# Two chained mixture-of-experts layers on one core: the branch on a job's width, the place of the output gates, the third gather and the row buffers are rewritten

## Chip, core and metric

One core of one Trainium2 chip. The metric is the device time of one launch in microseconds (us); several launches are timed and the median is used.

## What is computed

Local attention, then a mixture of 8 experts that routes by the largest logit, then a second mixture of 8 experts in which every expert takes exactly 576 tokens. All in float32; 4608 tokens, 512 columns, 1024 hidden columns. The reference, cut to the part around the change (the first expert layer):

```python
def _moe_ref(x, w_gate, w_output_gate, w1, w2):
    N, D = x.shape
    logits = x @ w_gate
    e_idx = np.argmax(logits, axis=1)
    logits_s = logits - logits.max(-1, keepdims=True)
    probs = np.exp(logits_s)
    probs /= probs.sum(-1, keepdims=True) + 1e-09
    gate_w = probs[np.arange(N), e_idx]
    eom = 1.0 / (1.0 + np.exp(-(x @ w_output_gate)))
    out = np.zeros((N, D), dtype=np.float32)
    for e in range(E):
        mask = e_idx == e
        h = np.maximum(x[mask] @ w1[e], 0.0)
        ye = h @ w2[e]
        out[mask] = gate_w[mask, None] * eom[mask, e, None] * ye
    return out
```

## The kernel before

The program has three stages. **Attention** walks over 36 blocks of 128 tokens, writes the rows to DRAM (`xs`), and beside it the router works out for each token its expert and a slot in a list (`route`, `plan`). The **first expert layer** works the list off in jobs: a job is one expert's block of tokens. The **second expert layer** (`moe2`) selects 576 tokens for each expert and runs the experts one after the other; the change leaves it alone.

**Jobs and widths.** Jobs 0 to 2 hold 256 tokens each and start before routing is complete. Jobs 3 to 10 take a full block of 256 and the rest of the same expert together, sorted by size, and are 512, 448, 384, 320 or 256 tokens wide. The width is known only when the router is done, so each of these jobs exists five times in the code, once for each width; one copy is called an arm here, arm 0 being 512 wide and arm 4 256 wide. Jobs from 11 on are 256 wide, one behind the other, each under a test whether there are that many jobs at all (`tail`). With the inputs timed here jobs 3 to 10 take arms 0, 1, 1, 2, 3, 3, 3, 4, and job 14 is the last.

**The branch.** `run` (L709) calls `arms` (L713), which writes a binary tree of tests on four numbers `wide[k]` (how many jobs are wider than a limit). Each engine holds these numbers in registers (L289 loads four of them and the number of jobs) and runs the tree for itself: a test whose body is taken goes on with the instruction behind it, otherwise it jumps to the other half. The five arms lie one behind the other in the code, arm 0 first; at the end of an arm each engine jumps to what follows the fifth arm. There `evac` (L878) copies the last quarter of the output out of PSUM, and the next job's tests follow.

**Inside a job.** `layer1` (L832) multiplies by w1: eight parts f, each 4 x 3 matmuls (every float32 operand is split into a high and a low half, `whi`/`wlo`, `xhi`/`xlo`, `hhi`/`hlo`). ACT makes `hhi` (L849), DVE `hlo` (L850). After every quarter a hook runs: it splits chunks of w2 (`split`, L694: ACT `whi` L697, DVE `wlo` L698) and fetches the same chunk of the next job's w1 into the raw buffer that came free (`fetch`, L687, a DMA issue on SP, L691). `layer2` (L859) multiplies by w2 in three groups of output quarters, and at the places given by `TODO` it splits the next job's w1, fetches the next job's w2 and turns and splits the next job's rows (L824, L829, L830).

**Gathers.** `x_load` (L811) works out row numbers on DVE (`idx`, L816) and issues indirect DMAs on POOL (L818) that gather a job's rows into `xr`. For jobs 1 and 2 it is called from a hook of the job before (L769), in job 0 at hook 0 and in job 1 at hook 1:

```python
            if i == (1 if j else 0) and j < EARLY - 1:
                self.x_load(n)
```

**Gates.** `gate(j-1)` (L886) is a generator that runs during `layer1` of job j, one step for every three matmuls. It multiplies the finished output `yT` by the second layer's gate weights (L894), copies that (`gT`, L896), turns it (L904), sets down logits and choices (`place`, `choose`: small DVE operations), and turns the output rows with DVE (`rows`: `y`, L916), each of two or four `y` followed by four stores to DRAM on SP (L919, `x<-y`). Its first step is one `yield`, so its first matmuls stand behind six matmuls of `layer1`. `y` comes from a pool with two buffers: the third transpose of a job waits until the stores of the first have landed.

PE, DVE, ACT and SP run their instructions in the order in which this code calls them; each engine's queue is strictly in that order.

Of the kernel before, what the change touches and what calls it, by code (L numbers as in the profile page):

```python
# [8 lines left out]
F32 = mybir.dt.float32  # L9
# [28 lines left out]
CH = 1024  # L38
SURE = NJ - E
EARLY = 3  # L40
HOLD = 1
GFULL = E * (BT - 1) // (128 * G)
TH = 2 * BT
STEP = 64
NC = (TH - BT) // STEP
CAP = N // E
BIG = 1e38
HC = 100
# [20 lines left out]
class Kernel:  # L69
# [136 lines left out]
    def setup(self, st):  # L206
        nc, tc = self.nc, self.tc
        dram = self.ctx.enter_context(tc.tile_pool(name="dram", bufs=1, space=DRAM))
        self.xs = dram.tile([N, D], F32, name="xs")
        self.list = dram.tile([NB * BT, 2], F32, name="list")  # L210
        self.x2 = dram.tile([NB * BT, ROW], F32, name="x2")
        keep = self.ctx.enter_context(tc.tile_pool(name="keep", bufs=1))
        self.seed = keep.tile([128, 2 * EARLY], I32, name="seed")
        self.jobs = keep.tile([128, 3], I32, name="jobs")
        self.counts = keep.tile([128, NC + 1], I32, name="counts")
        self.L = keep.tile([128, NS, E], F32, name="L")
        self.m = keep.tile([128, NS], F32, name="m")
        self.C = keep.tile([128, NS, E], BF, name="C")
        self.first = keep.tile([128, NS, 16], BF, name="first")
        self.f = keep.tile([128, NS], F32, name="f")  # L220
        self.left = keep.tile([128, 1], F32, name="left")
        self.dead = keep.tile([128, NS], F32, name="dead")
        wpool = self.ctx.enter_context(tc.tile_pool(name="weights", bufs=1))
        self.raw = [wpool.tile([128, CH], F32, name=f"wr{i}") for i in range(4)]
        self.chunks = self.weights(wpool, 0)
        self.ps = st.enter_context(tc.tile_pool(name="psA", bufs=1, space=PSUM))
        self.turn = self.ring = 0
        self.later = []
        self.last = None
        fix = st.enter_context(tc.tile_pool(name="fix", bufs=1))  # L230
        self.xr = fix.tile([128, 4, D], F32, name="xr")
        self.blank = fix.tile([128, ROW], F32, name="blank")
        self.meta = [fix.tile([128, 4, 2], F32, name=f"meta{i}") for i in range(3)]
        self.xhi = fix.tile([128, 4, TH], F32R, name="xhi")
        self.xlo = fix.tile([128, 4, TH], F32R, name="xlo")
        self.tab = fix.tile([128, E, NJ], F32, name="tab")
        self.order = fix.tile([128, E, EARLY], F32, name="order")
        self.opened0 = fix.tile([128, E, NJ], F32, name="opened0")
        self.total0 = fix.tile([128, 1], F32, name="total0")
        self.acc0 = fix.tile([128, E], BF, name="acc0")  # L240
        self.mw = st.enter_context(tc.tile_pool(name="mw", bufs=2))
        self.wk = st.enter_context(tc.tile_pool(name="wk", bufs=2))
# [36 lines left out]
    def first_layers(self):  # L279
        nc, tc = self.nc, self.tc  # L280
        self.consts = self.ctx.enter_context(tc.tile_pool(name="consts", bufs=1))
        with ExitStack() as st:
            self.setup(st)
            with ExitStack() as sa:
                self.attention(sa)
            self.buffers(st)
            for j in range(EARLY):
                self.job(j, BT)
            *self.wide, self.count = (nc.values_load(self.counts[0:1, i:i + 1], min_val=0, max_val=E if i < NC else NB)  # L289
                                      for i in range(NC + 1))  # L290
            for j in range(EARLY, SURE):
                self.run(j)
                self.evac()
            self.tail(SURE)
# [324 lines left out]
    def plan(self, cnt, used):  # L619
# [38 lines left out]
        yield  # L658
        V.tensor_reduce(pos, big, axis=AX.X, op=OP.add)
        V.tensor_scalar(cn[:, NC:], cn[:, NC - 1:NC], float(EARLY), None, op0=OP.add)  # L660
        V.tensor_copy(self.counts[:, 0:NC], cn[:, 0:NC])
        yield
        V.scalar_tensor_tensor(ct, pos[:, :, None].to_broadcast(sj), EARLY + 1.0, t1, op0=OP.add, op1=OP.mult)
        cp = wk.tile(sj, F32, name="pcp", bufs=1)
        V.tensor_tensor_scan(cp.rearrange(jf), pr.rearrange(jf), pr.rearrange(jf), initial=cn[:, NC:],
                             op0=OP.add, op1=OP.bypass)
        yield
        V.tensor_copy(self.counts[:, NC:], cp[:, E - 1, NJ - 1:NJ])
        V.tensor_tensor(cp, cp, pr, op=OP.mult)
        V.tensor_tensor(ct, ct, cp, op=OP.add)  # L670
        yield
# [36 lines left out]

    def run(self, j):  # L709
        self.last = self.ps.tile([128, TH if self.wideable(j) else BT], F32, name="tp2")  # L710
        self.arms(j, 0 if self.wideable(j) else NC, NC)

    def arms(self, j, lo, hi):  # L713
        if lo == hi:
            self.job(j, TH - STEP * lo)
            return
        k = (lo + hi) // 2
        with self.tc.If(self.wide[k] > j - EARLY) as cmp:
            self.arms(j, lo, k)
        with cmp.Else():  # L720
            self.arms(j, k + 1, hi)

    def tail(self, j):
        tc = self.tc
# [12 lines left out]
    def job(self, j, w):  # L737
# [21 lines left out]
        def hook1(i):  # L759
# [6 lines left out]
            elif j == EARLY - 2 and i == 3:  # L766
                while self.routes:
                    self.advance(1)
            if i == (1 if j else 0) and j < EARLY - 1:  # L769
                self.x_load(n)  # L770
            if i == 3:
                if EARLY - 2 <= j < NB - 2:
# [113 lines left out]
    def gate(self, j):  # L886
# [1 line left out]
        meta = self.meta[j % 3]  # L888
        n = 4 if self.wideable(j) else 2
        w = n * 128  # L890
        yield
        pg = self.ps.tile([128, w], F32, name="pg")
        for k in range(4):
            nc.tensor.matmul(pg[32 * k:32 * k + 32], self.wg2s[:, k, :], self.yT[:, k, 0:w], start=True, stop=True)  # L894
# [17 lines left out]

    def rows(self, u, s):
        nc = self.nc
        y = self.mw.tile([128, 4, 4, 32], F32, name="y")
        nc.vector.transpose(y, self.yT[:, :, u * 128:(u + 1) * 128].rearrange("p k (t g) -> p g k t", g=4))  # L916
        to = self.x2[s * 128:(s + 1) * 128, 0:D].rearrange("(t g) (q c) -> g q t c", g=4, q=4)
        for g in range(4):
# [504 lines left out]
```

## Time and profile before

| | |
|---|---|
| median of 3 launches | 1337.66 us (1333.54 to 1338.27) |
| profiled execution, its own time | 1333.46 us |
| span of its instructions | 1331.6 us |
| busy: PE, DVE, ACT, POOL | 87%, 58%, 37%, 14% of the span |
| mean granted TensorE clock | 0.926 of full speed |
| the chain that ended last | PE 57%, issue 14%, DVE 7%, DMA 5% |

The jobs of the first expert layer in that execution (PE's first matmul of the job, and how long PE had stood still before it):

| job | width | starts at us | PE idle before, us |
|---|---|---|---|
| 3 | 512 | 306.78 | 0.34 |
| 4 | 448 | 358.56 | 4.36 |
| 5 | 448 | 408.35 | 4.82 |
| 6 | 384 | 458.86 | 4.81 |
| 7 | 320 | 506.94 | 7.57 |
| 8 | 320 | 552.33 | 6.68 |
| 9 | 320 | 599.18 | 8.77 |
| 10 | 256 | 644.97 | 7.61 |
| 11 | 256 | 677.27 | 2.70 |

A row of a timeline gives start, duration, engine, line, operation, output and inputs, shape, count and, in brackets, how long the engine stood idle before it and what ended that; "issue" means that the engine waited for nothing that the profile shows. A clock of 1.0 is 2.4 GHz and 0.5 is 1.2 GHz. In the DMA view q8 and q14 are the queues that bring instructions: q8 moves 16 KB pieces and q14 8 KB pieces.

### The profile page before, as it was taken

How to read it: one execution, taken by the hardware profiler on the slowest of the kernel's cores; microseconds unless marked ns; L12 is line 12 of the kernel's file. 1: busy time of each engine (PE TensorE's matmuls, PEld its weight loads, DVE VectorE, ACT ScalarE, POOL GpSimd, SP SyncE). 2: the span in 40 equal slices, each digit the busy share in tenths (PEclk: the TensorE clock that was granted, in tenths of full speed). 3: DMA queues.
4: the chain of work that ended last, by engine and by line, in shares of the span. 5: the costliest groups of instructions: out<-in, count | busy, mean ns of one | idle time of the engine just before them, and what ended most of it. 6: DMA issues, size and time to landing. Idle time of an engine off the chain costs nothing.

```text
span 1331.6 us, 23258 instructions
## 1 busy us (share of the span) xinstructions
PE 1157.2 (87%) x8424; PEld 998.5 (75%) x8424; DVE 776.3 (58%) x2214; ACT 489.6 (37%) x1052; POOL 192.7 (14%) x233
## 2 busy tenths in 40 slices
PE   6978789689898896769789963999999999999997
PEld 4766568688697796768689952878797878788895
DVE  4756687855254354345366667767787868654430
ACT  4655454334242243234244421323232323334430
POOL 3112243111101101110000101020202021112001
PEclk8978789899998897888899975899999999999999
DMA  6776867765353554564467652241515052434310
GB/s 207 235 180 203 202 204 152 198 204 143 109 163 105 151 168 107 161 193 112 123 181 226 206 152 91 76 143 60 168 35 194 14 190 73 138 96 148 114 48 36
DMA packets 90581, 190.06 MB, mean 143 GB/s; under 512 B 22992, under 2 KB 46608, under 8 KB 90384
## 3 DMA queue, kind: packets, MB, share of 16 engines
q1 hardware_dynamic: 77904, 153.96, 39.9%
q0 software_dynamic: 11136, 32.59, 7.7%
q8 instruction: 97, 1.59, 0.6%
q10 hardware_dynamic: 1344, 1.10, 0.3%
q14 instruction: 100, 0.82, 0.2%
HBM read 152.33 MB, written 35.28 MB: 141 GB/s over the span
## 4 chain that ended last, share of the span: by engine, by line
PE 57%; issue 14%; DVE 7%; DMA 5%; POOL 1%; ACT 1%; SPq 1%; ACTq 0%; another core or an unknown queue 0%; POOLq 0%; DVEq 0%
PE O L844 6%; PE ph L844 5%; PE ph L1289 4%; PE ph L1293 4%; PE ph L1291 4%; PE py L1326 3%; PE py L1324 3%; PE py L1328 3%; DMA wr<-in_w_dram 2%; PE O L867 2%; PE O L869 2%; PE O L868 2%; PE ph L867 2%; PE ph L869 2%; PE ph L868 2%
## 5 line engine op out<-in xcount | busy, mean ns | idle before, releaser
L698 DVE TENSOR_TENSOR wlo<-wr,whi 128x1024 fp32r<-128x1024 f32 x122 | 146.6, 1218 | 39.1 <-ACT whi L697 38.4
L1289 PE MATMUL ph<-xhi,whi 128*128 128x256 f32 (+1 forms) x512 | 155.6, 304 | 2.0 <-DVE hlo L1298 0.7
L697 ACT ACTIVATE whi<-wr 128x1024 fp32r<-128x1024 f32 x122 | 126.5, 1054 | 80.8 <-DMA wr<-in_w_dram 37.4
L1291 PE MATMUL ph<-xlo,whi 128*128 128x256 f32 (+1 forms) x512 | 154.7, 302 | 0.0
L1293 PE MATMUL ph<-xhi,wlo 128*128 128x256 f32 (+1 forms) x512 | 154.4, 302 | 0.0
L818 POOL DMA_INDIRECT xr<-xs,idx x48 | 46.3, 965 | 461.9 <-DVE idx L816 143.1
L844 PE MATMUL O<-xhi,whi 128*128 128x256 f32 (+4 forms) x240 | 79.8, 334 | 33.6 <-issue 33.6
L1326 PE MATMUL py<-wlo,hhi 128*128 128x512 f32 x256 | 105.2, 411 | 0.0
L1328 PE MATMUL py<-whi,hlo 128*128 128x512 f32 x256 | 103.0, 402 | 0.0
L1324 PE MATMUL py<-whi,hhi 128*128 128x512 f32 x256 | 102.7, 401 | 0.0
L1297 ACT ACTIVATE hhi<-ph 128x256 fp32r<-128x256 f32 x128 | 49.0, 384 | 145.3 <-PE ph L1293 140.6
L1289 PEld LDWEIGHTS ph<-xhi,whi 128*128 128x128 f32 x512 | 98.5, 192 | 3.9 <-issue 1.1
L1291 PEld LDWEIGHTS ph<-xlo,whi 128*128 128x128 f32 x512 | 98.7, 193 | 0.5 <-DVE xlo L1260 0.2
L1293 PEld LDWEIGHTS ph<-xhi,wlo 128*128 128x128 f32 x512 | 98.5, 192 | 0.4
L844 PE MATMUL ph<-xhi,whi 128*128 128x256 f32 (+4 forms) x240 | 76.8, 324 | 14.1 <-issue 11.4
L1245 DVE TENSOR_TENSOR wlo<-wr,whi 128x512 fp32r<-128x512 f32 x124 | 81.9, 684 | 8.1 <-ACT whi L1240 8.1
L1298 DVE SCALAR_TENSOR_TENSOR hlo<-ph,hhi 128x256 fp32r<-128x256 f32 x128 | 53.0, 419 | 51.5 <-ACT hhi L1297 33.3
L844 PEld LDWEIGHTS O<-xhi,whi 128*128 128x128 f32 x240 | 47.6, 198 | 45.6 <-issue 44.5
L844 PE MATMUL O<-xhi,wlo 128*128 128x256 f32 (+4 forms) x240 | 77.0, 323 | 0.0
L844 PE MATMUL ph<-xhi,wlo 128*128 128x256 f32 (+4 forms) x240 | 74.5, 314 | 0.0
L403 PE MATMUL ph<-qkv 128*64 128x128 f32 x576 | 47.4, 316 | 29.2 <-DMA qkv<-in_qkv_dram 28.5
L417 ACT ACTIVATE ex<-ph,nm 128x64 f32<-128x64 f32 x288 | 68.1, 346 | 11.7 <-DVE nm L410 10.1
(321 smaller groups left out, 2836.8 us busy)
## 6 DMA issues: line engine op xcount, KB each, us to landing
wr<-in_w_dram SPq DMA_DIRECT2D x128, 512.0 KB
qkv<-in_qkv_dram SPq DMA_DIRECT2D x72, 386.0 KB
wr<-in_w2b_dram SPq DMA_DIRECT2D x32, 512.0 KB
wr<-in_w1b_dram SPq DMA_DIRECT2D x30, 512.0 KB
x<-y SPq DMA_DIRECT2D x184, 64.0 KB
xs<-x SPq DMA_DIRECT2D x35, 256.0 KB
x<-blank SPq DMA_DIRECT2D x8, 514.0 KB
wr<-in_w1b_dram ACTq DMA_DIRECT2D x2, 512.0 KB
```

Of the source, the lines that this page charges most:

```text
L417: self.nc.scalar.activation(ex8[:, h // 2, h % 2, :], S8[:, h, :], AF.Exp, scale=0.125, bias=nm[:, h:h + 1])
L697: nc.scalar.activation(hi, self.raw[c], AF.Copy)
L698: (eng or nc.vector).tensor_tensor(lo, self.raw[c], hi.bitcast(F32), op=OP.subtract)
L844: nc.tensor.matmul(p[:, q, :], a[:, k, :], b[:, k, 0:w], start=c == 0, stop=c == 11)
L867: nc.tensor.matmul(q, whi[:, ds], self.hhi[:, f, 0:w], start=f == 0, stop=False)
L1245: self.nc.vector.tensor_tensor(lo[:, s], self.raw[c][:, s], hi[:, s].bitcast(F32), op=OP.subtract)
L1289: nc.tensor.matmul(p, whi[:, k, :], xhi[:, k, cs], start=k == 0, stop=False)
L1291: nc.tensor.matmul(p, whi[:, k, :], xlo[:, k, cs], start=False, stop=False)
L1293: nc.tensor.matmul(p, wlo[:, k, :], xhi[:, k, cs], start=False, stop=k == 3)
L1324: nc.tensor.matmul(p, hhi[:, f, ts], whi, start=f == 0, stop=False)
L1326: nc.tensor.matmul(p, hhi[:, f, ts], wlo, start=False, stop=False)
L1328: nc.tensor.matmul(p, hlo[:, f, ts], whi, start=False, stop=f == 7)
```

## The change

- **Branch.** The tree of tests is replaced by a chain. For each of jobs 3 to 10 a table `LIKELY` names two arms. The first test is "is it the first of these", with that arm directly behind it; the second the same for the second; the other three arms follow under a binary tree. The router now counts for each job which arm it takes (`arm`, two more DVE operations in `plan`), so every engine loads nine registers before job 3 where it loaded five; POOL loads its own one again before each job.
- **Third gather.** The gather of job 2's rows is called from hook 0 of job 1, where it was called from hook 1.
- **Gates.** `gate` waits six steps, where it waited one.
- **Rows.** `y` has four buffers, where it had two.

```diff
+GATE = 6
+LIKELY = (0, 1), (1, 0), (1, 2), (2, 1), (2, 3), (3, 2), (3, 4), (3, 4)
...
-            *self.wide, self.count = (nc.values_load(self.counts[0:1, i:i + 1], min_val=0, max_val=E if i < NC else NB)
-                                      for i in range(NC + 1))
+            *self.arm, self.count = (nc.values_load(self.counts[0:1, i:i + 1], min_val=0, max_val=NC if i < E else NB)
+                                     for i in range(E + 1))
...
-        V.tensor_copy(self.counts[:, 0:NC], cn[:, 0:NC])
+        V.tensor_tensor(arm, cn[:, None, 0:NC].to_broadcast(se), self.evec[:, :, 0:NC], op=OP.is_le)
+        V.tensor_reduce(arms, arm, axis=AX.X, op=OP.add)
+        V.tensor_copy(self.counts[:, 0:E], arms)
...
     def run(self, j):
-        self.arms(j, 0 if self.wideable(j) else NC, NC)
-
-    def arms(self, j, lo, hi):
-        if lo == hi:
-            self.job(j, TH - STEP * lo)
-            return
-        k = (lo + hi) // 2
-        with self.tc.If(self.wide[k] > j - EARLY) as cmp:
-            self.arms(j, lo, k)
+        if not self.wideable(j):
+            self.job(j, BT)
+            return
+        first = LIKELY[j - EARLY]
+        self.arms(j, self.arm[j - EARLY], first, [a for a in range(NC + 1) if a not in first])
+
+    def arms(self, j, arm, first, rest):
+        if not first and len(rest) == 1:
+            self.job(j, TH - STEP * rest[0])
+            return
+        k = len(rest) // 2
+        with self.tc.If(arm == first[0] if first else arm < rest[k]) as cmp:
+            if first:
+                self.job(j, TH - STEP * first[0])
+            else:
+                self.arms(j, arm, (), rest[:k])
         with cmp.Else():
-            self.arms(j, k + 1, hi)
+            self.arms(j, arm, first[1:], rest if first else rest[k:])
...
-            if i == (1 if j else 0) and j < EARLY - 1:
+            if i == 0 and j < EARLY - 1:
                 self.x_load(n)
...
-        yield
+        for _ in range(GATE):
+            yield
...
-        y = self.mw.tile([128, 4, 4, 32], F32, name="y")
+        y = self.mw.tile([128, 4, 4, 32], F32, name="y", bufs=4)
```

PE, where job 3 ends and job 4 begins. Before, three tests stand there and the 512 wide arm is behind them; job 4 takes the 448 wide arm, which lies behind that one:

```order
L869 MATMUL tp_4279<-hlo,whi_3090 128x256
L718 UNCONDITIONAL_BRANCH
L718 COMPARE_AND_BRANCH x3
L844 MATMUL O<-xhi,whi_85 128x512
L844 MATMUL O<-xhi,wlo_86 128x512
L844 MATMUL O<-xhi,whi_85 128x512
```

The same place now:

```order
L883 MATMUL tp_4339<-hlo,whi_3090 128x256
L729 UNCONDITIONAL_BRANCH
L729 COMPARE_AND_BRANCH
L858 MATMUL O<-xhi,whi_85 128x448
L858 MATMUL O<-xhi,wlo_86 128x448
L858 MATMUL O<-xhi,whi_85 128x448
```

One test is left, and the 448 wide arm follows it at once; the jump at the end of an arm is still there.

DVE in job 1, from the split of the first w2 chunk on; `idx<-meta_103` makes the row numbers of the third gather. Before (between these two pieces stand 19 more rows):

```order
L698 TENSOR_TENSOR wlo_3085<-wr_81,whi_3084 128x1024
L954 TENSOR_TENSOR cw_3587<-L,m 128x16
L955 TENSOR_TENSOR m<-m,dead 128x2
L960 TENSOR_TENSOR first<-m,thr_548 128x32
```

```order
L850 SCALAR_TENSOR_TENSOR hlo<-O,hhi 128x2x256
L698 TENSOR_TENSOR wlo_3087<-wr_82,whi_3086 128x1024
L698 TENSOR_TENSOR wlo_3089<-wr_83,whi_3088 128x1024
L816 TENSOR_SCALAR idx<-meta_103 128x2
L668 CAST counts<-pcp 128x1
```

Now:

```order
L705 TENSOR_TENSOR wlo_3085<-wr_81,whi_3084 128x1024
L830 TENSOR_SCALAR idx<-meta_103 128x2
L640 TENSOR_TENSOR ppr<-opened,pt_3558 128x144
L641 TENSOR_TENSOR ppr<-ppr,pfirst 128x144
L642 TENSOR_TENSOR ppr<-ppr,pt_3558 128x8x17
```

The row numbers moved from behind the third split to behind the first.

SP in job 8, 320 wide, during `layer1` (`wr` rows are fetches of the next job's w1, `x_64<-y` the stores of the rows). Before:

```order
L919 DMA x_64<-y 4x32x128 x4
L691 ISA
L691 DMA wr_81<-in_w_dram 128x1024
L919 DMA x_64<-y 4x32x128 x4
L691 ISA
L691 DMA wr_82<-in_w_dram 128x1024
L691 ISA
L691 DMA wr_83<-in_w_dram 128x1024
L919 DMA x_64<-y 4x32x128 x8
L691 ISA
L691 DMA wr_84<-in_w_dram 128x1024
```

Now:

```order
L934 DMA x_64<-y 4x32x128 x4
L698 ISA
L698 DMA wr_81<-in_w_dram 128x1024
L698 ISA
L698 DMA wr_82<-in_w_dram 128x1024
L698 ISA
L698 DMA wr_83<-in_w_dram 128x1024
L934 DMA x_64<-y 4x32x128 x8
L698 ISA
L698 DMA wr_84<-in_w_dram 128x1024
L934 DMA x_64<-y 4x32x128 x4
```

Four stores moved from ahead of the second fetch to behind it, and four from ahead of the last fetch to behind it.

## Rows read from the trace of the kernel before

**Rows 1.** Waits of PE, 340 to 800 us (us in total, times, longest)
```profile
PE O L844 <- issue: 33.6, 5, 8.8
PE ph L844 <- issue: 11.0, 2, 6.7
PE ph L867 <- DVE hlo L850: 5.2, 3, 2.6
PE O L867 <- DVE hlo L850: 2.4, 1, 2.4
PE ph L869 <- DVE hlo L850: 1.6, 1, 1.6
PE O L869 <- DVE hlo L850: 1.2, 1, 1.2
```

**Rows 2.** Timeline of PE, first matmul of jobs 3, 4, 7, 8, 9, 11
```profile
306.78 0.49 PE L844 MATMUL ph<-xhi,whi 128*128 128x512 f32 x1 [0.34 <-issue]
...
358.56 0.60 PE L844 MATMUL ph<-xhi,whi 128*128 128x448 f32 x1 [4.36 <-issue]
...
506.94 0.63 PE L844 MATMUL O<-xhi,whi 128*128 128x320 f32 x1 [7.57 <-issue]
...
552.33 0.62 PE L844 MATMUL ph<-xhi,whi 128*128 128x320 f32 x1 [6.68 <-issue]
...
599.18 0.63 PE L844 MATMUL O<-xhi,whi 128*128 128x320 f32 x1 [8.77 <-issue]
...
677.27 0.39 PE L844 MATMUL ph<-xhi,whi 128*128 128x256 f32 x1 [2.70 <-ACT yT L876]
```

**Rows 3.** DMA queues, 350.8 to 351.0 us (packets, MB, share of 16 engines)
```profile
q8 instruction: 1, 0.02, 29.8%
```

**Rows 4.** DMA queues, 354.0 to 354.2 us
```profile
q8 instruction: 1, 0.02, 51.3%
```

**Rows 5.** DMA queues, 591.0 to 591.2 us
```profile
q8 instruction: 1, 0.02, 33.5%
```

**Rows 6.** DMA queues, 594.4 to 594.6 us
```profile
q8 instruction: 2, 0.03, 138.9%
```

**Rows 7.** Windows: us, each engine's busy time (and count), PE clock, DMA share, GB/s
```profile
358.56:363.06 4.50, 4.50 (x17) 2.39 (x18) 0.00 (x0) 0.36 (x1) 0.35 (x1) 0.62 0.62 159
...
458.86:464.86 6.00, 6.00 (x21) 3.90 (x22) 0.00 (x0) 0.60 (x1) 2.12 (x3) 0.52 0.78 178
528.85:533.05 4.20, 4.20 (x19) 4.19 (x20) 4.20 (x6) 1.54 (x2) 0.00 (x0) 0.59 0.30 72
...
620.60:625.60 5.00, 5.00 (x25) 4.95 (x26) 5.00 (x7) 2.64 (x4) 0.00 (x0) 0.66 0.34 92
677.27:680.27 3.00, 3.00 (x23) 2.03 (x24) 2.28 (x5) 1.03 (x2) 0.94 (x1) 1.00 0.80 266
...
552.33:590.40 38.07, 35.62 (x220) 33.06 (x220) 19.33 (x34) 14.66 (x23) 2.36 (x3) 0.90 0.53 155
```

**Rows 8.** Waits of DVE, 205 to 785 us, and timeline of ACT in job 11
```profile
DVE y L916 <- DMA x<-y: 19.1, 7, 3.3
...
706.35 1.06 ACT L697 ACTIVATE whi<-wr 128x1024 fp32r<-128x1024 f32 x1 [6.04 <-DMA wr<-in_w_dram]
```

**Rows 9.** Timelines of DVE, POOL and PE in job 1, and PE in job 2
```profile
242.59 1.23 DVE L698 TENSOR_TENSOR wlo<-wr,whi 128x1024 fp32r<-128x1024 f32 x1 [0.25 <-ACT whi L697]
...
251.40 0.16 DVE L816 TENSOR_SCALAR idx<-meta 128x2 int32<-128x2 f32 x1
...
244.95 0.96 POOL L585 DMA_INDIRECT list<-xm,idx  x1 [0.30 <-issue]
252.33 0.97 POOL L818 DMA_INDIRECT xr<-xs,idx  x1 [6.43 <-issue]
...
260.30 1.12 PE L824 MATMUL tp<-ident,xr 128*128 128x128 f32 x4 [10.14 <-DMA xr<-xs,idx]
...
277.37 0.61 PE L904 MATMUL pg<-sel,gT 128*128 128x8 f32 x4 [1.01 <-ACT gT L896]
```

More of the change, by code (lines that the diff above doesn't have):

```diff
@@ L214, in setup @@
         self.jobs = keep.tile([128, 3], I32, name="jobs")
-        self.counts = keep.tile([128, NC + 1], I32, name="counts")
+        self.counts = keep.tile([128, E + 1], I32, name="counts")
         self.L = keep.tile([128, NS, E], F32, name="L")
@@ L660, in plan @@
         V.tensor_scalar(cn[:, NC:], cn[:, NC - 1:NC], float(EARLY), None, op0=OP.add)
-        V.tensor_copy(self.counts[:, 0:NC], cn[:, 0:NC])
+        se = [128, E, NC]
+        arm = wk.tile(se, F32, name="parm", bufs=1)
+        V.tensor_tensor(arm, cn[:, None, 0:NC].to_broadcast(se), self.evec[:, :, 0:NC], op=OP.is_le)
+        arms = wk.tile([128, E], F32, name="parms", bufs=1)
+        V.tensor_reduce(arms, arm, axis=AX.X, op=OP.add)
+        V.tensor_copy(self.counts[:, 0:E], arms)
         yield
@@ L667, in plan @@
         yield
-        V.tensor_copy(self.counts[:, NC:], cp[:, E - 1, NJ - 1:NJ])
+        V.tensor_copy(self.counts[:, E:], cp[:, E - 1, NJ - 1:NJ])
         V.tensor_tensor(cp, cp, pr, op=OP.mult)
```

## The prediction

> **What bounds the kernel now.** I went from the chain of waits on the page (PE 57%, "issue" 14%) to the waits of PE in the wide jobs, and from there to single starts. In [rows 1] the two "issue" lines are PE standing still in front of a job's first matmul, 33.6 + 11.0 = 44.6 us in seven stops, and the four `hlo` lines are PE standing still where `layer2` begins, 5.2 + 2.4 + 1.6 + 1.2 = 10.4 us. No other wait of PE in these jobs is near that size, so PE's stops set the length of this stage; what shortens them shortens the run.
>
> The stops at the job starts are code that has to be fetched. [Rows 2]: job 3 enters by falling through three tests into arm 0, and PE stood 0.34 us. Job 4 has to jump twice, out of arm 0 past four arms and then past arm 0 into arm 1, and PE stood 4.36 us. [Rows 3, 4] show two 16 KB instruction packets in this stop, at 350.8 and 354.0; [rows 5, 6] show those of job 9, at 591.0 and 594.4. The second request comes 3.2 and 3.4 us after the first, which is how long one jump holds PE's instruction stream; the matmul follows some 4.5 us behind the second packet. In job 4 the first packet lies ahead of PE's stop (358.56 - 4.36 = 354.20), because matmuls were still queued; in job 9 it lies behind PE's stop (590.41), so the whole pair shows, 8.77 us.
>
> A stop also costs clock. [Rows 7]: after job 4's stop 4.50 us ran at 0.62 (1.2 GHz for most of it), which loses 4.50 x 0.38 = 1.7 us against 2.4 GHz; after job 6's 6.00 x 0.48 = 2.9 us. After the 2.70 us stop of job 11 the clock was 1.00.
>
> The `hlo` stops come from the row buffers. [Rows 8]: DVE waited 19.1 us in seven waits for stores `x<-y` before it could overwrite `y`, and `hlo` is queued on DVE behind that transpose.
>
> **The change, part by part.** All sums are against the profiled execution, 1333.46 us; the median of the runs is 4.2 us above it.
>
> *Branch.* Jobs 3 to 6, 8 and 9 take the arm that now stands first, jobs 7 and 10 the second. Job 3 entered without a jump already. For jobs 4, 5, 6, 8 and 9 the jump into the arm goes and the jump out of the last arm stays, as the order shows: one fetch less each. The bound from below is half of job 4's stop, 2.2 us, from above the whole of it, 4.4; I take the spacing of the packets, 3.3, which measures this very thing: 5 x 3.3 = **-16.5 us**. What is left of the stops is then 4.36 - 3.3 = 1.1 us in job 4, much the same in 5 and 6 (4.82 and 4.81), 3.4 in job 8 and 5.5 in job 9. A stop near 1.1 us is well under the 2.70 that left the clock alone, so the half-speed stretches of jobs 4 to 6 go: 3 x 2.3 (mean of 1.7 and 2.9) = **-6.9 us**. In jobs 8 and 9 I leave them. Jobs 7 and 10 had one jump out and at least one in, and have that still: 0.
>
> Job 11 loses something. Job 10 took arm 4, the last, and fell out of it; now that arm is second of five and its end is a jump over three. The stop of job 11 was 2.70 us and waited for ACT, which itself waited for a weight chunk; I put what is left in jobs 8 and 9 in its place, (3.4 + 5.5) / 2 = 4.4, so +1.7, and the clock of 2.3 with it: **+4.0 us**. Ends: 0, if the loss hides in that wait, and +6.
>
> Four more register loads stand on each engine before job 3. Five loads and three tests left 0.34 us there [rows 2]; four more cost no more than that again if the queue still covers them: **+0.3**. The Trainium skill, in Runtime: NRT & Kernel Launch, section Instruction fetch mechanics, gives some 200 ns for each register loaded, which would be 0.8 in its place; no row here shows a single load.
>
> *Row buffers and gates.* With four buffers no transpose within a job waits for a store of that job. The ends are 10.4 us (all four lines of [rows 1]) and 4, if DVE's own work holds `hlo`: the gates now begin five steps later, and one more transpose stands behind the third split. I take **-9.0 us**. Three of these stops cost clock too, in [rows 7] 4.20 x 0.41 = 1.7 us for the first and 5.00 x 0.34 = 1.7 for the last: **-5.1 us**. The later gates are hidden under `layer1`; they are needed now, since in a job that starts at once the gates' matmuls, six matmuls in, would wait for `evac`. Job 2 has such a wait, for `gT`, 1.01 us [rows 9]: **-1.0 us**. On SP four stores move behind the fetches of the second and third chunk and four behind the last, so no weight chunk comes later by that; in [rows 8] ACT stood 6.04 us for such a chunk in job 11, which leaves room for it.
>
> *Third gather.* [Rows 9]: POOL issued its last scatter from 244.95 to 245.91, then stood still until `idx` was done behind the third split (251.40) and issued the gather at 252.33; PE had stopped 10.14 us when the rows came at 260.30. `idx` now follows the first split, which ends at 243.82, so the gather can go 0.3 us behind the last scatter, at 246.2: **-6.1 us**. Some 4 us of the stop stay, and with them the half clock behind it. Ends: -4, if the transfer takes longer beside the weights, and -7.
>
> Sum: -16.5 - 6.9 + 4.0 + 0.3 - 9.0 - 5.1 - 1.0 - 6.1 = -40.3, so 1293.2 beside the profiled execution, and **1297 us** as a median. What is late next is job 7's and 10's pair of fetches and the weight chunks of the narrow jobs.
>
> **Rivals.**
>
> *The weights take part of it back.* Jobs of 320 and 256 columns gave their weights the stops to arrive in. If each of jobs 8 to 11 then waits 4 us more for a chunk (two thirds of the 6.04), 16 us come back: 1313. Against it: in [rows 7] the DMA engines were busy 0.53 of job 8's time, and the fetches now stand earlier on SP. Chance 0.16.
>
> *A test at the target of a jump costs a fetch even when it is not taken.* Job 7 jumps out, jumps to a test and falls through that into arm 3, and stood 7.57 us, where job 4 stood 4.36. Then the five fetches and the clock of jobs 4 to 6 do not go (+23.4), and jobs 7 and 10 meet one more such test (+6.6): 1327. Against it: job 4 also falls through two tests at its first target, and its packets stand no farther apart than those of job 9, which takes its first test at once; what differs is how much queued work covered the first fetch. Chance 0.07.
>
> *A jump over one arm finds its target already loaded.* Job 8 shows what an arm is, 220 matmuls and 220 weight loads [rows 7], 440 instructions. Jobs 7 and 10 would then lose one fetch each, 2 x 3.3: 1290. Against it: job 8 left arm 3 over arm 4 alone, just such a jump, and [rows 5] shows the fetch for it. The section of the Trainium skill named above says that only a jump to outside the current two blocks of 256 instructions stalls, which taken at its word is this rival; that packet speaks against it. Chance 0.04.
>
> *Slower: the stores crowd out the fetch of the last w1 chunk.* With four buffers up to sixteen stores of a job are let go without waiting, eight of them ahead of that fetch. If the chunk then lands a whole wait later, 6.04 us of ACT, ahead of the copies that free PSUM for PE, and brings the half clock (2.2), each of jobs 4 to 11 pays 8.2 us, 66 in all: 1297 + 66 = 1363. It decides against the change once a job pays more than 5 us. For it speaks that ACT and DVE both waited for DMA in [rows 8]; against it, that four stores left the place ahead of the fetch. Chance 0.03.
>
> **How the numbers follow.** My forecast has 0.68; it and the four rivals make 0.98, the rest is open. For the range, the lower ends together are -22 (fetches), -11.5 (clock, jobs 8 and 9 with it), -10.4, -5.1, -7 and -1, or -57: 1281 as a median; the upper ends -11, -3, -4, -1.7, -4, +6 and +0.8, or -17: 1321. I give 1279 to 1320, which leaves out the slower rival and most of the one on tests. A measurement of this kernel can tell about 0.5% from no change, 6.7 us. Faster by more than that are the forecast, the weights, the short jump and, at 1327, the tests: 0.93 with what is uncertain in them; within it 0.04; slower 0.03.
>
> **What would show it.** PE's stop before jobs 4, 5 and 6 near 1 us with the clock at 1.00 after it, and one 16 KB packet in it; jobs 8 and 9 near 3 and 5 us; jobs 7 and 10 as before; job 11 longer than 2.70. No wait of DVE `y` for `x<-y`. The gather of job 2 near 246 us and PE's wait for it near 4. I am wrong if jobs 4 to 6 still stand over 3 us, if PE waits for weight chunks in jobs 8 to 11, or if `hlo` still holds `layer2`.

## The result, and the profile after

| | before | changed | ratio (95%) |
|---|---|---|---|
| first set of launches | 1335.6 us (4) | **1270.98 us** (4, 1267.11 to 1277.62) | 0.9528 (0.9470 to 0.9585) |
| second set (e9) | 1333.93 (11) | 1283.41 (5) | 0.9614 (0.9588 to 0.9640) |
| third set (e13) | 1325.68 (11) | 1274.27 (6) | 0.9617 (0.9585 to 0.9648) |

The first set counts: 1271, 64.6 us less. I had said 1297, 40.3 us less, with 1279 as the lower end. The sign and the places were right, the size was not. The other two sets, run on two different chips, gave 50.5 and 51.4 us less. The profiled execution took 1268.38 us. The page after:

```profile
span 1266.6 us, 23227 instructions
...
PE 1136.8 (90%) x8424; PEld 987.4 (78%) x8424; DVE 777.4 (61%) x2216; ACT 489.1 (39%) x1052; POOL 196.1 (15%) x233
...
PE 55%; issue 12%; DVE 7%; DMA 3%; POOL 1%; ACT 1%; another core or an unknown queue 1%; SPq 0%; POOLq 0%; ACTq 0%; DVEq 0%
```

PE's waits in the wide jobs of the changed kernel (340 to 730 us), the counterpart of [rows 1]:

```profile
PE ph L858 <- issue: 11.7, 2, 9.5
PE O L858 <- issue: 10.8, 2, 7.7
PE pg L909 <- issue: 3.6, 1, 3.6
...
PE pg L909 <- ACT yT L890: 1.2, 1, 1.2
```

"Issue" in front of `ph` and `O` fell from 44.6 to 22.5 us, and no `hlo` line of the first layer is among the large ones any more. The single starts, counterpart of [rows 2] (first matmuls of jobs 4 to 11; no bracket means that PE did not stand):

```profile
335.92 0.37 PE L858 MATMUL O<-xhi,whi 128*128 128x448 f32 x1
378.96 0.44 PE L858 MATMUL ph<-xhi,whi 128*128 128x448 f32 x1
421.97 0.41 PE L858 MATMUL O<-xhi,whi 128*128 128x384 f32 x1
466.92 0.63 PE L858 MATMUL O<-xhi,whi 128*128 128x320 f32 x1 [7.68 <-issue]
503.94 0.39 PE L858 MATMUL O<-xhi,whi 128*128 128x320 f32 x1 [3.07 <-issue]
540.10 0.39 PE L858 MATMUL ph<-xhi,whi 128*128 128x320 f32 x1 [2.14 <-issue]
582.88 0.57 PE L858 MATMUL ph<-xhi,whi 128*128 128x256 f32 x1 [9.52 <-issue]
612.12 0.36 PE L858 MATMUL ph<-xhi,whi 128*128 128x256 f32 x1 [1.67 <-ACT yT L890]
```

Jobs 4 to 6 start without a stop (in the second and third profile of this kernel they stand at most 1.03 us). The DMA queues in the windows 332.4 to 332.8 (ahead of job 4) and 376.0 to 376.4 (job 5), and then 575.2 to 575.6 and 578.4 to 578.8 (job 10, which still jumps twice):

```profile
q8 instruction: 1, 0.02, 14.6%
q8 instruction: 1, 0.02, 16.5%
...
q8 instruction: 1, 0.02, 14.7%
q8 instruction: 1, 0.02, 18.3%
```

The packet of job 4 comes 3.1 to 3.5 us ahead of its matmul, that of job 5 2.6 to 3.0, and PE is busy all that time: one jump is hidden whole under queued matmuls. In job 10 the second packet follows some 3 us behind the first, the matmul 4.1 to 4.5 behind that.

The trace also records the jumps themselves: a taken branch on PE's queue lasts until the code behind it runs (ahead of job 4 in the kernel before it ends at 358.50, the first matmul starts at 358.56). The middle number of a row is its duration in ns. The kernel before, ahead of job 4: the jump out of job 3's arm, then the jump into job 4's. The changed kernel: the jump ahead of job 4, then the one ahead of job 8.

```profile
L718 PEldq COMPARE_BRANCH  x1: 3309/3309/3309, 350.0 to 350.0; - x1
L718 PEldq COMPARE_BRANCH  x1: 4892/4892/4892, 353.6 to 353.6; - x1
...
L729 PEldq COMPARE_BRANCH  x1: 3269/3269/3269, 331.9 to 331.9; - x1
L729 PEldq COMPARE_BRANCH  x1: 5551/5551/5551, 498.1 to 498.1; - x1
```

The first jump of the pair and the lone one of job 4 took the same 3.3 us, the second of the pair took 4.9. What a jump costs is what sticks out from under the queued matmuls: the one ahead of job 4 began 4.1 us before that job's first matmul and PE was busy throughout; the one ahead of job 8 began 2.8 us before PE's last queued matmul ended (500.87), so of its 5.6 us some 2.8 were bare, and PE stood 3.07.

Windows of 4 us behind the starts of jobs 7, 8, 9, 10 and 11 (columns as in [rows 7]; the clock stands third from the right):

```profile
466.92:470.92 4.00, 4.00 (x17) 4.00 (x18) 0.00 (x0) 0.42 (x1) 0.00 (x0) 0.60 0.43 91
503.94:507.94 4.00, 4.00 (x17) 4.00 (x18) 0.15 (x1) 0.44 (x1) 2.72 (x3) 0.57 1.03 406
540.10:544.10 4.00, 4.00 (x29) 3.21 (x29) 1.80 (x4) 0.44 (x1) 2.26 (x3) 1.00 1.00 399
582.88:586.88 4.00, 4.00 (x21) 4.00 (x21) 0.00 (x0) 0.00 (x0) 0.00 (x0) 0.59 0.18 41
612.12:616.12 4.00, 4.00 (x32) 3.02 (x33) 0.59 (x1) 0.28 (x2) 0.00 (x0) 1.00 0.96 278
```

The stop of 3.07 us cost as much clock (4.00 x 0.43 = 1.7 us) as that of 9.52 (1.6). Those of 2.14 and 1.67 cost none. That is no clean limit: in other profiles stops of 1.76 (e6, job 11), 2.01 (e7, job 11) and 2.31 us (e9, job 8) cost 1.7 us too, where the 2.70 of [rows 2] cost nothing.

The third gather, counterpart of [rows 9], POOL and PE in job 1:

```profile
236.05 0.96 POOL L587 DMA_INDIRECT list<-xm,idx  x1 [0.30 <-issue]
237.32 0.98 POOL L832 DMA_INDIRECT xr<-xs,idx  x1 [0.30 <-issue]
...
245.10 1.11 PE L838 MATMUL tp<-ident,xr 128*128 128x128 f32 x4 [2.37 <-DMA xr<-xs,idx]
```

**Where the time went.** For every profile I cut the jobs into windows of half a us: a window less PE's busy time is idle time, PE's busy time x (1 - clock) is clock lost. All in us; "starts" are PE's stops in front of jobs 4 to 11.

| profile | job 0 at | jobs 1+2 | jobs 3 to 14 | of it starts | other idle | clock lost |
|---|---|---|---|---|---|---|
| before | 209.9 | 70.1 | 475.4 | 47.3 | 11.7 | 21.8 |
| before, e14 | 204.5 | 70.0 | 477.5 | 45.9 | 13.4 | 23.5 |
| changed | 201.1 | 60.6 | 427.1 | 24.1 | 3.3 | 5.0 |
| changed, e9 | 207.3 | 66.3 | 433.0 | 27.2 | 3.7 | 7.4 |
| changed, e13 | 202.9 | 59.7 | 433.8 | 28.6 | 2.6 | 8.8 |
| e1 chain alone | 207.1 | 72.6 | 443.4 | 21.1 | 14.7 | 12.8 |
| e2 rows and gates alone | 207.3 | 67.1 | 467.7 | 56.3 | 1.3 | 16.9 |
| e3 gather alone | 202.7 | 66.0 | 477.4 | 49.0 | 13.6 | 19.7 |
| e5 all but the chain | 202.6 | 57.7 | 464.9 | 55.9 | 1.4 | 14.5 |
| e6 five jumps more | 204.8 | 62.8 | 469.9 | 52.3 | 5.1 | 19.0 |
| e7 all but the gather | 205.9 | 65.9 | 429.7 | 26.0 | 2.5 | 7.1 |
| e8 as e5, no weights | 207.7 | 60.8 | 450.0 | 41.4 | 1.6 | 14.2 |
| e11 gates at once | 203.1 | 69.0 | 444.0 | 30.9 | 5.6 | 13.9 |
| e15 two row buffers | 208.8 | 60.9 | 460.4 | 23.0 | 26.5 | 17.6 |
| exact table, e4 / e10 / e16 | 204.6 / 202.8 / 197.1 | 63.9 / 64.3 / 62.8 | 423.7 / 427.2 / 427.4 | 16.3 / 19.4 / 19.1 | 4.5 / 4.3 / 4.6 | 8.6 / 8.9 / 9.8 |
| e12 exact, no weights | 205.4 | 64.5 | 408.1 | 6.6 | 4.8 | 3.0 |

The two first profiles differ by 65.0 us: 48.3 in jobs 3 to 14, 9.4 in jobs 1 and 2 and 8.7 ahead of job 0, less 1.5 behind job 14. The mean of three changed profiles against that of two before gives 45.1 and 7.9; my terms for these places sum to 33.2 and 7.1.

### The profile page after: what moved, and what is told of

It reads as the page before. It is cut to its first block, busy times and chain, and to the rows that moved or that the text cites. A ratio compares the mean times of both kernels' runs of the same rounds, so it can differ in the third digit from the quotient of the medians.

```text
span 1266.6 us, 23227 instructions
## 1 busy us (share of the span) xinstructions
PE 1136.8 (90%) x8424; PEld 987.4 (78%) x8424; DVE 777.4 (61%) x2216; ACT 489.1 (39%) x1052; POOL 196.1 (15%) x233
## 4 chain that ended last, share of the span: by engine, by line
PE 55%; issue 12%; DVE 7%; DMA 3%; POOL 1%; ACT 1%; another core or an unknown queue 1%; SPq 0%; POOLq 0%; ACTq 0%; DVEq 0%
PE ph L858 7%; PE O L858 6%; PE ph L1304 4%; PE ph L1306 4%; PE ph L1308 4%; PE py L1341 3%; PE py L1339 3%; PE py L1343 3%; PE s L1021 2%; PE O L881 2%; PE O L883 2%; PE O L882 2%; DVE wlo L705 2%; PE py L1326 2%; PE ph L881 2%
## 5 line engine op out<-in xcount | busy, mean ns | idle before, releaser
L705 DVE TENSOR_TENSOR wlo<-wr,whi 128x1024 fp32r<-128x1024 f32 x122 | 146.9, 1223 | 41.4 <-ACT whi L704 40.5
L704 ACT ACTIVATE whi<-wr 128x1024 fp32r<-128x1024 f32 x122 | 126.1, 1054 | 75.2 <-DMA wr<-in_w_dram 38.4
L858 PE MATMUL ph<-xhi,whi 128*128 128x256 f32 (+4 forms) x240 | 75.4, 320 | 15.1 <-issue 13.4
L858 PE MATMUL O<-xhi,whi 128*128 128x256 f32 (+4 forms) x240 | 76.5, 321 | 10.8 <-issue 10.8
L419 ACT ACTIVATE ex<-ph,nm 128x64 f32<-128x64 f32 x288 | 68.0, 347 | 13.8 <-DVE nm L412 11.5
L858 PE MATMUL O<-xlo,whi 128*128 128x256 f32 (+4 forms) x240 | 71.9, 316 | 1.0 <-issue 1.0
L1255 ACT ACTIVATE whi<-wr 128x1024 fp32r<-128x1024 f32 x62 | 64.8, 1053 | 12.5 <-DMA wr<-in_w1b_dram 11.1
```

The lines of the kernel that those rows point to most:

```text
L419: self.nc.scalar.activation(ex8[:, h // 2, h % 2, :], S8[:, h, :], AF.Exp, scale=0.125, bias=nm[:, h:h + 1])
L704: nc.scalar.activation(hi, self.raw[c], AF.Copy)
L705: (eng or nc.vector).tensor_tensor(lo, self.raw[c], hi.bitcast(F32), op=OP.subtract)
L858: nc.tensor.matmul(p[:, q, :], a[:, k, :], b[:, k, 0:w], start=c == 0, stop=c == 11)
L1255: self.nc.scalar.activation(self.chunks[4 * w + c][0], self.raw[c], AF.Copy)
```

## Experiments

**The price of a jump.** e6 takes the changed kernel and turns the table round:

```diff
-LIKELY = (0, 1), (1, 0), (1, 2), (2, 1), (2, 3), (3, 2), (3, 4), (3, 4)
+LIKELY = (0, 1), (0, 1), (2, 1), (1, 2), (2, 3), (2, 3), (4, 3), (3, 4)
```

> The changed kernel with the table turned round, so that all eight jobs take the arm that stands second: one jump more in jobs 3, 4, 5, 6, 8 and 9. Theory A (a jump costs 3.3 us, the spacing of two packets, and 2.3 us of clock where PE had not stood before): 6 x 3.3 + 4 x 2.3 = 29 us more than the changed kernel, 1300. Theory B (a jump behind a jump can't be hidden, it costs the 4.5 us from its packet to the first matmul): 6 x 4.5 + 4 x 1.7 = 34, 1305; jobs 4 to 6 stand 4.4 to 6 us, jobs 8 and 9 7 to 10. Rival (a jump over one arm alone finds its target loaded): jobs 4 to 6 stand under 1 us and the time is that of the changed kernel.

In the kernel that ran, job 3 kept its first hit, so the jumps added are five, in jobs 4, 5, 6, 8 and 9, not six. 1316.57 us, 0.9882 of before (0.9834 to 0.9931), slower than either theory had it. The starts of those jobs in e6:

```profile
346.68 0.46 PE L858 MATMUL ph<-xhi,whi 128*128 128x448 f32 x1 [4.67 <-issue]
396.69 0.73 PE L858 MATMUL O<-xhi,whi 128*128 128x448 f32 x1 [5.29 <-issue]
445.52 0.43 PE L858 MATMUL ph<-xhi,whi 128*128 128x384 f32 x1 [3.38 <-issue]
540.06 0.63 PE L858 MATMUL ph<-xhi,whi 128*128 128x320 f32 x1 [9.63 <-issue]
584.16 0.62 PE L858 MATMUL O<-xhi,whi 128*128 128x320 f32 x1 [9.32 <-issue]
```

Against the mean of the three changed profiles the starts grew by 25.7 us and the clock lost by 11.9: 5.1 and 2.4 us a jump, where I had 3.3 and 1.4 (6.9 over five). In jobs 4 and 5 the added jump lasted 5.0 and 4.7 us and two 16 KB packets came during it; in job 6 it lasted 3.4 us, with one packet. The rival of the short jump falls: jobs 4 to 6 jump over one arm, and stood 3.4 to 5.3 us. The Trainium skill, Runtime: NRT & Kernel Launch, section Instruction fetch mechanics, says that a taken branch fetches when its target is outside the current window of two pages. The trace agrees if that window is the block of the jump and the next one: an arm (440 instructions in job 8 of the kernel before) is 1.7 blocks of 256, so from most places in a block the jump ends beyond the next.

e5 is the changed kernel with the tree of tests (`run` and `arms` of the kernel before). e8 is e5 without weights:

```diff
-                if more:
+                if more and j < EARLY:
                     self.fetch(c, self.w1, self.reg)
...
-        self.fetch(c, self.w2, self.reg)
+        if j < EARLY:
+            self.fetch(c, self.w2, self.reg)
```

> The changed kernel with the old tree of tests (four row buffers, six steps, gather from hook 0 stay). Theory A (my forecast's price of the chain, 19 us): about 1290. Theory B (the chain is worth more beside four row buffers than beside two, because without the hlo stops PE reaches the jumps with less queued and more data in flight, as the stops of 5.7 to 10.1 us in jobs 5 to 10 of the kernel with rows and gates alone suggest): the starts of jobs 4 to 10 stand 50 us or more together and the run takes about 1310. If the chain is worth the same 29 us beside either, 1300.

> As the kernel with the tree and the other parts (sent with it), but from job 3 on the weights of the first expert layer are not fetched: the old ones are split and used again, the DMA traffic of the jobs falls to the rows and the code. Theory B (code that is fetched beside weights comes later): the starts of jobs 7 to 10 fall from 9 to 10 us to 7 or less, jobs 4 to 6 (384 columns and more) lose under 1 us each. Rival (a fetch of code takes its time whatever the DMA engines move): every start within 1 us of its twin.

e5: 1313.15 us, 0.9845 (0.9806 to 0.9884), near the 1310 of theory B, but not for its reason: the chain turns out to be worth the same beside either number of buffers (below). e8: one launch, 1295.55. The stops before jobs 7 to 10 as windows, e5 first (PE's busy time is 0; the DMA share is the last number but one):

```profile
479.91:489.38 9.47, 0.00 (x1) 0.01 (x1) 0.38 (x2) 0.60 (x1) 3.79 (x4) 0.66 0.81 242
523.57:533.23 9.66, 0.00 (x1) 0.01 (x1) 0.39 (x2) 0.60 (x1) 3.79 (x4) 0.69 0.89 313
567.67:577.62 9.95, 0.00 (x1) 0.01 (x1) 0.39 (x2) 0.60 (x1) 3.79 (x4) 0.70 0.95 307
612.06:621.75 9.69, 0.00 (x1) 0.03 (x1) 1.33 (x3) 0.60 (x1) 1.90 (x2) 0.71 0.68 208
```

and e8:

```profile
487.75:494.20 6.45, 0.00 (x2) 0.01 (x1) 0.22 (x1) 0.60 (x1) 2.16 (x3) 0.74 0.55 158
528.32:534.62 6.30, 0.00 (x1) 0.01 (x1) 0.22 (x1) 0.60 (x1) 1.90 (x2) 0.77 0.67 159
568.95:575.36 6.41, 0.00 (x2) 0.01 (x1) 0.22 (x1) 0.60 (x1) 2.88 (x4) 0.80 0.64 167
609.82:616.79 6.97, 0.00 (x1) 0.03 (x1) 1.13 (x2) 0.60 (x1) 0.00 (x0) 0.78 0.35 98
```

Without weights these four stops are 12.6 us shorter together; those of jobs 4 to 6 are 15.2 against 15.8. So code fetched beside data comes later, 3.2 us for a pair of jumps, as theory B says. The kernel before had these stops at 6.7 to 8.8 us and a DMA share of 0.44 to 0.58 in them.

**The parts alone.** e1 is the changed kernel with the other parts undone (`GATE = 1`, the gather's hook as before, `y` without `bufs=4`); e2 is the kernel before with six steps ahead of the gates and `bufs=4`; e3 is the kernel before with the gather's new hook.

> The chain alone, with one yield ahead of the gates, the third gather from hook 1 and two row buffers, as before. Theory A (my forecast's prices): five fetches of 3.3 us go, three half-clock stretches of 2.3 us go, job 11 loses 4.0: about 19 us less than before. Theory B (the profile of the changed kernel): one jump that is left hides wholly under queued matmuls, so jobs 4 to 6 lose their whole stop (14.0 us) and jobs 8 and 9 lose 3.6 and 6.6, the clock of jobs 4 to 6 is 7.1, job 11 loses nothing: about 31 us less. Rival C (the parts need each other: with only two row buffers layer2 is held longer once jobs start at once): less than 15 us, and more wait of PE for hlo than the 10.4 us of [rows 1].

> Four row buffers and six steps ahead of the gates, on the tree of tests and the old gather. Theory A: 10.4 us of hlo stops less 1.4, and 5.1 of clock and 1.0 of gT: about 15 us less than before. Theory B: the hlo stops also held the clock of jobs 7 to 9 down (9.4 us less lost there in the changed kernel), so about 10 + 8 to 9 = 18 to 20 us less. If the 8.7 us by which job 0 starts earlier in the changed kernel come from where the buffers lie, job 0 starts near 198 here too; if they are drift between executions, it starts anywhere between 197 and 207 in any of these kernels.

> The third gather from hook 0 alone. Theory A: 6.1 us less than before, the half clock behind the stop of job 1 stays. Theory B: 6.7 us of the stop and 3 to 6 us of job 2 (its wait of 2.96 us for xlo and 3.0 us of half clock behind it, which the changed kernel doesn't have): 9 to 12 us less. If job 2's gain belongs to the gates instead, 6 to 7.

e1: 1308.04 us, 0.9785 (0.9719 to 0.9851), 28.9 us less and near B. e2: 1319.98, 0.9840 (0.9766 to 0.9913), 17.0 less, between A and B. e3: 1330.84, 0.9968 (0.9926 to 1.0009), 6.1 less, which by its interval can be nothing. In jobs 3 to 14 the chain alone takes 33.0 us off, and 33.6 where the rest is there (e5 against the changed kernel). Rows and gates take 8.7 off alone and 11.5 in e5. e3 leaves jobs 3 to 14 as they were. So the parts add up, and rival C falls, though one half of its sign came: in e1 PE stood 12.4 us for `hlo`. What rows and gates free in `hlo` is partly given back at the starts, which grow by 9.7 us in e2:

```profile
PE O L844 <- issue: 41.0, 5, 10.1
PE ph L844 <- issue: 14.2, 2, 9.5
```

**The parts undone.** e7 is the changed kernel with the old hook for the gather, e11 with `GATE = 1`, e15 with `y` of two buffers.

> The changed kernel with the third gather back at hook 1. Theory A: 6.1 us more than the changed kernel, 1277. Theory B: job 2's wait for xlo and its half clock come back too, 9 to 12 us more, 1281. If the gates hid it, no more than 3.

> The changed kernel with one yield ahead of the gates as before; four row buffers stay. Theory A (my forecast: with jobs that start at once the gates' first matmuls, six matmuls in, wait for the last copy out of PSUM): up to 1 us in each of jobs 2 to 14, 3 to 12 us more than the changed kernel. Rival (the gates were worth nothing, the buffers did it all): within 3 us of it, and no wait of PE for yT in front of pg.

> The changed kernel with two row buffers; the gates stay six steps late. Theory A and B alike: the transposes wait for stores again and hlo holds layer2, 10 us of stops and 5 to 9 of clock, so 15 to 19 us more than the changed kernel. Rival (the later gates alone took hlo out of the way, since the gates at once cost 7 to 20 us): under 5 us more.

e7: 1280.63 us, 0.9609 (0.9562 to 0.9655), a ratio like the changed kernel's in the second and third sets; in its profile jobs 1 and 2 are 3.7 us longer than the changed kernel's mean. In the run's time the gather is worth a few us at most; what it does to PE is plainer. PE waited 10.1 to 12.7 us for the third gather's rows in the five profiles with the old hook (before, e14, e1, e2, e7) and 1.8 to 7.2 us in the thirteen with the new one. e11: 1290.84 us, 0.9698 (0.9650 to 0.9745), 7.4 us over the changed kernel of its set; jobs 1 and 2 took 69.0. Early gates take back what the early gather gives: in e3 and e11, which have both, PE stands 6.0 and 6.1 us for `xlo` in job 2, in the kernels with late gates 0.5 to 2.2. PE's waits in e11 (230 to 743 us) show what the early gates hold up:

```profile
PE tp L838 <- DVE xlo L844: 8.1, 4, 6.1
PE ph L858 <- ACT yT L890: 4.9, 1, 4.9
...
PE pg L909 <- ACT yT L890: 3.6, 1, 3.6
```

The first line is job 2, the second the start of job 11, the third job 12. The wait of `pg` that I had expected in every job came in this one alone; the rest of the 11 us by which jobs 3 to 14 are longer than in e9 lies in the starts and the clock.

e15: 1299.80 us, 0.9802 (0.9769 to 0.9835), 25.5 us over the changed kernel of its set and more than the 15 to 19 expected. PE's waits in e15 (290 to 760 us):

```profile
PE tp L838 <- DVE xlo L844: 19.8, 6, 5.5
...
PE ph L883 <- DVE hlo L864: 6.8, 2, 3.5
```

and DVE's:

```profile
DVE y L931 <- DMA x<-y: 35.6, 8, 5.0
```

With the gates late and two buffers the transposes wait beside the next job's splits, and `xlo` is what they hold. e1, with two buffers and early gates, took 443.4 us in jobs 3 to 14, e15 460.4: late gates without the buffers cost 17 us, by one profile each, of which e15's was the longest of its five launches.

**The same kernels again.** e9 and e13 are the changed kernel, e14 the kernel before.

> The changed kernel once more, unaltered, beside the kernel with the exact table. Theory B holds that the 8.7 us by which its job 0 started earlier than in the kernel before are drift between executions: job 0 then starts somewhere between 201 and 210 us, the stage from job 0 to the end of job 14 takes 514.6 within 5 us, and the median lies between 1268 and 1277. If the early start belongs to the change, job 0 starts under 203 again.

> The changed kernel a third time. If the first timing was a favourable set (job 0 early by 6 us and job 1 short by 7 us against the second profile), the median lies between 1275 and 1286; if the second was unfavourable, between 1267 and 1275. Either way jobs 3 to 14 together take 450 to 462 us (453.9 and 459.9 so far).

> The kernel before, unaltered, for a second profile. If job 0's start at 209.88 in the first profile was drift, it now lies anywhere between 201 and 209; jobs 1 and 2 together take 66 to 74 us (70.1 in the first); jobs 3 to 14 take 475.4 within 4 us, because their stops are the same at each execution.

e9 missed two of its three ranges: job 0 started at 207.3, inside, but the median was 1283.4 (1268 to 1277) and the stage from job 0 to the end of job 14 took 526.2 us (514.6 within 5), of it 5.9 more in jobs 3 to 14 and 5.7 in jobs 1 and 2 than in the first profile, where PE waited 7.2 us for the third gather's rows instead of 2.4. e13's 1274.3 lies in the lower of its two ranges. e14 lies inside all of its own. The range for "jobs 3 to 14" in e13's text counted job 0 in by mistake; with it e13 took 460.7, inside. The start of job 0 lay between 197.1 and 208.8 us in the profiles of the experiments, whichever parts they had, and at 204.5 in e14, and no instruction ahead of job 0 was changed: the 8.7 us between the first two profiles are spread between launches. Jobs 3 to 14 repeat within 2.1 us (before) and 6.7 us (changed).

**The arm that is taken, first in all jobs.** e4, e10 and e16 are one kernel, e12 is that without weights (the edit of e8):

```diff
-LIKELY = (0, 1), (1, 0), (1, 2), (2, 1), (2, 3), (3, 2), (3, 4), (3, 4)
+LIKELY = (0, 1), (1, 0), (1, 2), (2, 1), (3, 2), (3, 2), (3, 4), (4, 3)
```

> The changed kernel with the table naming the arm that is taken first for all eight jobs, so that no job jumps into its arm. Theory B (a stop with one jump is what is left when the queued matmuls are done): job 7 stands at most 3.1 us where it stood 7.68 and job 10 some 2.5 where it stood 9.52, and 1.6 us of half clock behind each goes: 11.6 + 2 to 3.3, so 13 to 15 us less than the changed kernel, about 1257. Rival D (the weights of the narrow jobs then come too late): PE waits for split chunks in jobs 8 to 11 and less than 7 us are gained.

> The exact table once more, beside the changed kernel. Theory D (what the two jumps give is taken back by weights that come later, 4.55 us at job 10 and 1.8 in job 12 in the first profile): within 5 us of the changed kernel. Theory B: 13 to 15 us less, the first timing being chance.

> The exact table a third time. Theory B (a jump that goes gives back its stop): 11 to 15 us less than the changed kernel of the same set. Theory D (weights take it back): within 5 us of it.

> The exact table, and from job 3 on no weights of the first expert layer are fetched (the old ones are split again). Theory D: PE's waits for yT at job 10 (4.55 us) and in job 12 (1.80) go, the stops of jobs 7 to 10 are 1 to 3 us, and jobs 3 to 14 lose under 15 us to idle and clock together, where the exact table with weights lost 33. Rival (ACT's own jumps hold it): job 10 still stands over 4 us.

1272.10 us (e4: 0.9508, 0.9446 to 0.9570), 1269.68 (e10: 0.9523, 0.9496 to 0.9551) and 1267.88 (e16: 0.9570, 0.9530 to 0.9611). Beside the changed kernel of the same set that is 13.7 us less in the second and 6.4 in the third; e4 had none beside it, and against the first timing, from another set, it showed no gain. The intervals of e13 and e16 overlap, so the size of the gain stays open. It is the fastest kernel here, but the table then fits these inputs. Theory B's jumps do go: the starts of jobs 7 and 10 fell from 8.50 and 9.84 (e9) to these of e10,

```profile
468.98 0.38 PE L858 MATMUL ph<-xhi,whi 128*128 128x320 f32 x1 [3.08 <-issue]
...
585.60 0.47 PE L858 MATMUL O<-xhi,whi 128*128 128x256 f32 x1 [4.64 <-ACT yT L893]
```

while the starts between them grew to 3.84 and 5.12. e12, one launch, 1254.9 us, shows that the weight fetches take it back: without them all starts together are 6.6 us, the clock loses 3.0, and the start of job 10 reads

```profile
570.28 0.36 PE L859 MATMUL O<-xhi,whi 128*128 128x256 f32 x1 [1.46 <-ACT yT L894]
```

They do it by delaying the code; theory D had the weights themselves come late. The lone jump ahead of job 8, e10 first, then e12:

```profile
L729 PEldq COMPARE_BRANCH  x1: 6317/6317/6317, 500.2 to 500.2; - x1
L729 PEldq COMPARE_BRANCH  x1: 3657/3657/3657, 498.3 to 498.3; - x1
```

The four jumps ahead of jobs 7 to 10 last 6.0 to 7.6 us in e10 and 3.6 to 3.9 in e12, 11.9 us together, beside 12.8 by which all starts differ; PE's first matmul stands 0.3 to 0.5 us behind the end of its own jump in all of them. Of the 19 us between e10 and e12 in jobs 3 to 14, 5.9 are clock. The other idle of PE, in which a late chunk would show, is 4.3 to 4.6 us with the weights and 4.8 without.

## Why the prediction was wrong

**The chain's price: the step that failed.** I took "the spacing of the packets, 3.3, which measures this very thing", and left 1.1 us of the stop in jobs 4 to 6. The spacing is how long the first of two jumps lasts (3.3 us ahead of job 4). But that one is hidden under queued matmuls, in jobs 4 to 6 whole; the one behind it is bare, and lasts 4.8 to 5.0 us in jobs 4 to 6. Take one away and the other is hidden, so the whole stop goes, the upper end of my bounds: in e1 the starts of jobs 4 to 6 fell from 14.0 to 0.2 us, and those of jobs 8 and 9 by 9.6 together; over the five that is 4.7 a jump. From packet to matmul a lone jump took 3.5 us at most (jobs 4 and 5), not the 4.5 that I read behind the second of a pair. I had also read two 16 KB packets into job 4's stop; a third comes 0.6 us behind the second (354.6), and the two packets in [rows 6] are the same thing in job 9. Why most second jumps bring two packets, and whether that is what makes them longer, was not tried; the one in e6's job 6 that brought one lasted 3.4 us. The chain was forecast at -16.5 - 6.9 + 4.0 + 0.3 = -19.1; alone it gave -33.0 in jobs 3 to 14, some 25 in the starts and 10 in the clock. That is 13.9 more, and the whole of the 11.9 (45.1 - 33.2) by which jobs 3 to 14 missed; rows and gates gave some 2 less than I said.

**The clock** of jobs 4 to 6 came out right: 7.1 us lost before, none after, forecast 6.9. In part that was luck: the stops that I thought short enough, near 1.1 us, were 0 here, and a stop of 1.76 us cost clock elsewhere (e6). In jobs 7 to 10 it fell from 14.6 (4.4 + 3.9 + 4.4 + 2.0) to 5.0 (1.6 + 1.7 + 0 + 1.65), where I counted 5.1 and left the starts' share alone.

**Job 11's 4.0 us** did not come in the changed kernel: its start took 1.67, 1.67 and 1.79 us and cost no clock. The jump that I feared is there (3.7 us in the first profile), but 2.3 us of it lie under queued matmuls. With the chain alone (e1) half of my price came: 3.16 us and 1.7 of clock.

**The register loads** were sized too small, as 0.3: job 3 starts behind a stop of 1.7 to 1.8 us in every kernel with the chain and 0.34 to 0.37 in every kernel with the tree. That is 1.4 for four loads more and two tests fewer. I wrote that no row shows a single load; the trace of the kernel before does, and this is its row:

```profile
L289 PEldq TENSOR_LOAD <-counts x5: 306/312/496, 304.1 to 306.0; - x5
```

A load takes 0.31 us, and they start 0.41 apart; four more are 1.6, less 0.26 for two tests. The five loads before were covered by matmuls queued until 306.44, the four more were not. The Trainium skill's 200 ns a register (Runtime: NRT & Kernel Launch, Instruction fetch mechanics), 0.8 for four, would have been nearer than my 0.3, but is under what the trace shows.

**Row buffers and gates** came out near, 2 to 5 us too high: forecast -9.0 - 5.1 in jobs 3 to 14, measured 8.7 (e2) and 11.5 (e5) on the tree and some 12 beside the chain. But the sum hides two larger numbers: 11 to 12 us of other idle and 6 to 8 of clock go, and 5 to 10 come back as longer starts, which I did not count. DVE no longer waits for `x<-y` before `y` at all (19.1 us before), and `hlo` holds PE 0.3 us.

**Jobs 1 and 2**: forecast -7.1, measured -7.9 as a mean. The gather left 0.3 us behind the last scatter, as I said, and PE waited 2.4, 7.2 and 3.0 us for its rows in the three profiles, not 10.1; I had said 4. The wait for `gT` stayed in the first profile (1.27) and was gone in the other two.

**Rivals.** In the changed kernel the weights took nothing visible: what PE waited for ACT's copies at jobs 11 and 12, 1.67 and 1.23 us, was there before (2.70 and 0.9). Their fetches cost by delaying the code (e12), which none of my rivals had. A test at a jump's target costs no fetch: jobs 4 to 6 would have stood. No stop of PE for a crowded chunk came.

**The range.** All lower ends together made 57 us, and jobs 1 to 14 of the first profile gave 48.3 + 9.4 = 57.7: nearly every term lay at its end. What carried the time past 1279 is the start of job 0, 8.7 us earlier, for which the range had no term: the spread between launches, up to 12 us between the medians of one kernel. The second set (1283.4) lies in the range, the third (1274.3) doesn't, but there the kernel before was 10 us shorter too. Taken as differences, my range was 18 to 59 us less: the 50.5 and 51.4 of the later sets lie inside, the 64.6 of the first outside. So the first set was a favourable one; but jobs 4 to 6 start almost without a stop in all three profiles, so the chain's price was too low in each.

## What to carry to other kernels

Price a stop with several fetches by what is left when one is gone, worked out from its start in the queue, not by the spacing of requests: the part that work covers belongs to the jump that stays. Look for the branches and register loads themselves in the trace (their source line on the engine's queue), where their durations stand. Put the likely case directly behind the test, and count what a freed stage then sends through the DMA engines at the moment in which code is fetched. Compare variants only within one set of launches: the same kernel's median moved by 12 us between sets, which ran on different chips.

## What I had not expected of the hardware

Code that is fetched beside data comes later: a lone jump took 6.0 to 7.6 us ahead of jobs 7 to 10 beside the weight fetches and 3.6 to 3.9 without them (e10, e12), and a pair of jumps stood 9.5 to 10.0 us at a DMA share of 0.68 to 0.95 and 6.3 to 7.0 us at 0.35 to 0.67 (e5, e8). And the clock does not follow the length of a stop: one of 3.07 us cost as much as one of 9.52, about 1.7 us, one of 1.76 did too, and one of 2.70 cost nothing.
